# Three more first layer blocks on split data, and the order of loads and sums around them

## Chip, cores and metric

One core of one Trainium2 chip runs the kernel as a single launch. The metric is the device time of that launch in microseconds (us), lower is better. The kernel before takes 1257.91 us (median of three runs).

## The reference, cut to what matters

Three stages: a linear attention with a decaying state, then a mixture of four two-layer ReLU networks weighted per token, then one two-layer network with g = h cos h.

```python
for t in range(S):                                   # 768 steps, 4 sequences x 8 heads, head size 48
    cur = einsum('bhd,bhe->bhde', u * k[:, :, t], v[:, :, t])
    y[:, :, t] = einsum('bhd,bhde->bhe', r[:, :, t], state + cur)
    state = w[..., None] * state + einsum('bhd,bhe->bhde', k[:, :, t], v[:, :, t])
x = y as 3072 tokens x 384
for e in range(4):                                   # w1: 384 x 1024, w2: 1024 x 384
    out += p[:, e:e+1] * (maximum(x @ w1[e], 0) @ w2[e])
h = out @ w_in                                       # 384 x 2048
return (h * cos(h)) @ w_out                          # 2048 x 384
```

## The kernel before, in words

The 3072 tokens are six tiles of 512. The hidden units of both networks are cut into blocks of 128. An **item** is one block on one token tile: an up product (384 to 128, three matmuls over `kk`, lines 619 to 630), an activation, and a down product (128 to 384, three matmuls, lines 701 to 705). Eight items make a unit and accumulate in three PSUM tiles `a0` to `a2`, which VectorE evicts with the token probabilities `pb` (lines 722 and 725). The main loop runs over the item number `n` from 0. In loop step `n` stand the up product of item `n` and the down product of an item two before (`lag`); item 8's down product, in step 10, is the first to write `a0` to `a2` anew, so it needs them evicted.

Products are taken in two ways. A *split* item keeps each float32 operand as two parts, high and low (`xh`, `xl`; `w[:, 0]`, `w[:, 1]`; `gh`, `gl`), and each matmul is three: high by high, high by low, low by high. A *plain* item multiplies the float32 data as it was loaded (`raw_w`, `x_raw`). Only items 0 to 7, the first eight first layer blocks on half a token tile (256 columns), can be plain; `SPLIT` names those of them that aren't. The parts of a weight tile are made by ScalarE (high, line 522) and by VectorE or GpSimd (low, line 526), in `w_split`; those of the first tokens by `split` (lines 117, 118).

The up products go in turn to two PSUM tiles `hp0` and `hp1`. An item's up product can start when the activation of the item two before has been read out of the same tile: `gh` by ScalarE (lines 637, 641), and for split items `gl` by VectorE (line 642). The attention's matmuls use the same tiles: `a_visit` in step `n` writes into the one that item `n` doesn't use, `ups2[1 - item[0] % 2]`.

The attention is worked through in 24 cells of 128 steps of one sequence. Cells 0 and 1 come before the loop; cell `c` from 2 on is begun in step `ONE_AT[c]` (3, 6, 10, 14, ...). Its preparation is a list of steps in `steps_of`: loads `a_load_tok`, `a_load_t`; `a_ru`, `a_kt` on GpSimd; `a_r`, `a_rk`, `a_kp`, `a_sum` on VectorE. `BEGIN` holds the cells whose loads and `a_ru` don't follow the rule. `mix` places these steps between the matmuls of an item. The attention's output goes to DRAM (`yd`, line 419) and comes back transposed (`x_in`, line 432), and is split into `xh`, `xl` from the list `later`.

The order on every engine is written by hand (`tc.manual_schedule`), so each engine and each DMA queue takes its instructions in program order. DMAs are issued by SyncE (SP) or ScalarE; an issue that has to wait holds up all that stands behind it in that queue. Two orders matter here:

- The raw blocks of items 0 to 7 have tiles of their own. The first six are loaded by SP ahead of the loop, the seventh and eighth by ScalarE in steps 3 and 4.
- Later weight tiles (`w_keys`) go through `st_p`, which has three buffers `s`. `w_loads(k)` issues loads up to the k-th, `w_splits(k, eng)` splits up to the k-th. In steps 3 to 7 these stand at the head of a step, `w_loads(n - 1)` and `w_splits(n - 3, ...)`. The load of a tile has to wait until the tile three before it has been split.

```python
            if 3 <= n < BLK:
                w_loads(n - 1)
                w_splits(n - 3, nc.gpsimd if n % 2 else None)
...
            if n == 7:
                prob_get(0, 0)
```

`prob_get` (line 858) loads the first `pb`; it stands behind the `w_loads` of step 7 in SP's queue.

Of the kernel before, what the change touches and what calls it, by code (L numbers as in the profile page):

```python
# [26 lines left out]
def attention_moe_cos_mlp_kernel(  # L27
# [17 lines left out]
    nc = tc.nc  # L45
# [79 lines left out]
    def a_load_t(c):  # L125
        b, i = cells[c]
        t = ld_p.tile([128, 2, HP, 128], F32, tag="rkt", name="rkt", bufs=4)
        (nc.scalar if N_FIRST < c < 6 else nc.sync).dma_start(out=t, in_=rkt[b, i])
        ld.setdefault(c, {})["t"] = t
# [21 lines left out]

    def a_ru(c):
        for ch in range(2):
            t = ld[c]["tok"][:, ch]
            nc.gpsimd.tensor_tensor(out=t, in0=t, in1=uu_ch[:, ch], op=ALU.mult)
# [10 lines left out]
    def a_kp(c):  # L166
        t, k0 = kps[c % 3], 1 if c < N_FIRST else 2
        nc.vector.tensor_tensor(
            out=t.rearrange("q (a p d) -> q a p d", a=2, d=D), in0=ld[c]["tok"][:, k0:k0 + 2], in1=wk_ch, op=ALU.mult,
        )  # L170
        ld[c]["kp"] = t
# [263 lines left out]
    def x_split(src, j, lag, cols=slice(0, TB), step=None):  # L435
        for kk in range(KD):
            later.append((
                lag + (step or X_STEP)[kk],
                lambda kk=kk: split(xh[j][:, kk, cols], xl[j][:, kk, cols], src[:, kk, cols]),
            ))  # L440

# [21 lines left out]
    BEGIN = {3: ((a_ru, 3),), 4: ((a_load_tok, 3), (a_load_t, 4), (a_ru, 5)), 5: ((a_load_tok, 6), (a_load_t, 7), (a_ru, 8))}  # L463

    def steps_of(c):
        at, p = ONE_AT[c], ONE_AT[c - 1]
        wide = at - p > 3
        two = ONE_AT.get(c - 2, 0)
        yield from BEGIN.get(c, ((a_load_tok, two - 1), (a_load_t, two), (a_ru, p - (2 if wide else 1))))
        yield from ((a_kt, p), (a_r, p + wide), (a_rk, p + 2), (a_kp, p + 2), (a_sum, p + 2 + wide))  # L470
# [278 lines left out]
    later = []  # L749
    NEXT = {(0, False): (2, 0), (1, False): (5, 1), (2, True): (0, 0), (3, True): (1, 2)}  # L750
# [124 lines left out]
    SPLIT = (4, 5)  # L875
# [45 lines left out]
    with tc.manual_schedule():  # L921
# [16 lines left out]
        raw_load(5)  # L938
        prob_load()
# [42 lines left out]
        for n in range(NI + 4):  # L982
            live = n < NI
            moe2 = False
            if 2 < n < 5:
                raw_load(n + 3, nc.scalar)
            if 3 <= n < BLK:
                w_loads(n - 1)
                w_splits(n - 3, nc.gpsimd if n % 2 else None)
            if n == 1:  # L990
                pt = table()
                for a in range(2):
                    table2(pt, a)
                for c in range(N_FIRST + 1):
                    a_kp(c)
# [62 lines left out]
            if n < N_ATT:  # L1058
                extra += steps.pop(n, [])
            for d in [x for x in later if x[0] <= 0]:  # L1060
                extra.append((on_pe_call, d[1]))
            later = [(x[0] - 1, x[1]) for x in later if x[0] > 0]
            mix(main, extra)
            for f in ends:
                f()
            if n == 1:
                for f in (a_load_tok, a_load_t):
                    f(N_FIRST + 1)
                w_split((0, 0, SPLIT[0]), nc.gpsimd, True)
            if n == 2:  # L1070
                w_loads(1)
                for kk in range(KD):
                    split(*(t[0][:, kk, 0:N_FIRST * 128].rearrange("q (c t) -> q c t", c=N_FIRST) for t in (xh, xl)), x_raw[:, :, kk, :])
                w_split((0, 0, SPLIT[1]), nc.gpsimd, True)
            if live:
                g = unit_at[ps, un]
                if n >= BLK:
                    w_splits(min(BLK * (g + 1) + w_ahead(n, g), n - 3 if n < BLK + 3 else len(w_keys)), nc.gpsimd if n < 28 and n % 2 else None)
# [219 lines left out]
```

## Time and profile before

| what | us |
|---|---|
| runs | 1256.98, 1257.91, 1258.26 |
| the profiled execution's own time | 1257.54 |
| its span | 1255.8 |
| PE busy | 1245.1 (99%) |
| PEld busy | 1038.3 (83%) |
| DVE busy | 765.7 (61%) |
| ACT busy | 491.6 (39%) |
| POOL busy | 228.3 (18%) |

PE is TensorE's matmuls and PEld its weight loads, DVE is VectorE, ACT ScalarE, POOL GpSimd, SP SyncE; ACTq and SPq are the DMA issues of a queue. The span is first to last instruction; 1.7 us of the profiled execution's time lie around it. L619 is line 619. In a timeline row the first number is the start in us from the span's start, the second the length, and a bracket gives the engine's idle time just before and what ended it.

### The profile page before, as it was taken

To read this page: it belongs to the slowest core of one execution; us is meant where nothing else is said; L and a number is where in the kernel's file an instruction comes from. 1 tells how busy PE (TensorE), PEld (TensorE's weight loads), DVE (VectorE), ACT (ScalarE), POOL (GpSimd) and SP (SyncE) were. 2 spreads that over 40 slices of the span, in tenths; PEclk is the share of its full clock that TensorE was granted. 3 is DMA by queue.
4 is the path that set the end of the run, shared out by engine and by line. 5 is a ranking of instruction groups with operands and counts; after the bars stand their busy time and mean duration, and the time that the engine had idled before them with its cause. 6 is when DMAs were issued, how large, how long until landed. Compare 5 with 4: busy or idle time off the path is not lost.

```text
span 1255.8 us, 20628 instructions
## 1 busy us (share of the span) xinstructions
PE 1245.1 (99%) x8465; PEld 1038.3 (83%) x8465; DVE 765.7 (61%) x1265; ACT 491.6 (39%) x881; POOL 228.3 (18%) x307
## 2 busy tenths in 40 slices
PE   9999999999999999999999999999999999999997
PEld 6998888888888888888888888888888888888886
DVE  7887746766265464547645642226777677777665
ACT  5442312223211131112111221126776777766774
POOL 5885324521100000111111111122000000010100
PEclk9999999999999999999999999999999999999999
DMA  8745534344231343223321410123001400160601
GB/s 312 233 125 177 192 122 156 124 142 132 80 112 64 97 134 97 74 70 130 113 83 52 142 34 9 59 99 103 1 1 51 151 26 26 45 203 5 200 11 44
DMA packets 72502, 126.54 MB, mean 101 GB/s; under 512 B 23153, under 2 KB 44754, under 8 KB 72402
## 3 DMA queue, kind: packets, MB, share of 16 engines
q1 hardware_dynamic: 66066, 94.56, 23.6%
q0 software_dynamic: 4608, 25.17, 6.2%
q10 hardware_dynamic: 1728, 5.44, 1.3%
q8 instruction: 67, 1.10, 0.4%
q14 instruction: 33, 0.27, 0.1%
HBM read 101.90 MB, written 23.25 MB: 100 GB/s over the span
## 4 chain that ended last, share of the span: by engine, by line


## 5 line engine op out<-in xcount | busy, mean ns | idle before, releaser
L628 PE MATMUL hp<-xh,w 128*128 128x512 f32 (+1 forms) x894 | 343.1, 384 | 0.1
L629 PE MATMUL hp<-xl,w 128*128 128x512 f32 (+1 forms) x894 | 340.2, 380 | 0.0
L630 PE MATMUL hp<-xh,w 128*128 128x512 f32 (+1 forms) x894 | 339.9, 380 | 0.0
L703 PE MATMUL a<-gh,w 128*128 128x512 f32 (+1 forms) x886 | 337.6, 381 | 0.1
L704 PE MATMUL a<-gh,w 128*128 128x512 f32 (+1 forms) x886 | 336.9, 380 | 0.0
L705 PE MATMUL a<-gl,w 128*128 128x512 f32 (+1 forms) x886 | 336.8, 380 | 0.0
L641 ACT ACTIVATE gh<-hp 128x512 fp32r<-128x512 f32 (+1 forms) x202 | 114.9, 569 | 533.8 <-PE hp L630 528.3
L642 DVE SCALAR_TENSOR_TENSOR gl<-hp,gh 128x512 fp32r<-128x512 f32 (+1 forms) x202 | 132.4, 655 | 293.8 <-ACT gh L641 292.9
L628 PEld LDWEIGHTS hp<-xh,w 128*128 128x128 f32 x894 | 168.1, 188 | 33.2 <-DVE gl L642 0.3
L630 PEld LDWEIGHTS hp<-xh,w 128*128 128x128 f32 x894 | 168.1, 188 | 31.8
L629 PEld LDWEIGHTS hp<-xl,w 128*128 128x128 f32 x894 | 168.2, 188 | 31.2
L703 PEld LDWEIGHTS a<-gh,w 128*128 128x128 f32 x886 | 166.7, 188 | 32.7 <-DVE pm L725 0.7
L705 PEld LDWEIGHTS a<-gl,w 128*128 128x128 f32 x886 | 166.7, 188 | 31.6
L704 PEld LDWEIGHTS a<-gh,w 128*128 128x128 f32 x886 | 166.7, 188 | 31.5
L727 POOL TENSOR_TENSOR acc<-acc,pm 128x256 f32<-128x256 f32 x108 | 87.9, 849 | 520.3 <-DVE pm L725 520.3
L661 DVE SCALAR_TENSOR_TENSOR hs<-rr,hs 128x512 f32<-128x512 f32 x96 | 66.9, 697 | 62.6 <-ACT rr L660 62.6
L659 ACT ACTIVATE rr<-rr 128x512 f32<-128x512 f32 x96 | 60.8, 633 | 87.6 <-DVE rr L654 87.6
L653 DVE SCALAR_TENSOR_TENSOR rr<-ni,hs 128x512 f32<-128x512 int32 x96 | 66.9, 697 | 45.7 <-ACT ni L652 45.7
L530 POOL DMA_DIRECT2D w<-dec_all x32 | 17.1, 535 | 330.8 <-PE a L705 330.8
L654 DVE SCALAR_TENSOR_TENSOR rr<-ni,rr 128x512 f32<-128x512 int32 x96 | 66.9, 697 | 3.3
L118 DVE TENSOR_TENSOR gl<-hs,gh 128x512 fp32r<-128x512 f32 x96 | 65.6, 684 | 0.7 <-ACT gh L117 0.7
L651 ACT ACTIVATE hs<-hp 128x512 f32<-128x512 f32 x96 | 57.1, 595 | 17.9 <-PE hp L630 17.7
(169 smaller groups left out, 1068.7 us busy)
## 6 DMA issues: line engine op xcount, KB each, us to landing
w<-dec_all POOLq DMA_DIRECT2D x32, 768.0 KB, 4.5
s<-in_moe_wb_dram SPq DMA_DIRECT2D x53, 384.0 KB, 4.2
draw<-in_moe_wb_dram SPq DMA_DIRECT2D x32, 384.0 KB, 3.8
dec_all<-dout SPq DMA_DIRECT2D x32, 384.0 KB, 3.0
tok<-in_tok_ch_dram SPq DMA_DIRECT2D x19, 576.0 KB, 5.6
rkt<-in_rkt_dram SPq DMA_DIRECT2D x21, 512.0 KB, 3.6
pb<-pn SPq DMA_DIRECT2D x24, 256.0 KB, 5.0
out_dram<-acc SPq DMA_DIRECT2D x17, 256.0 KB, 2.8
```

Source lines behind the costliest of these rows:

```text
L628: nc.tensor.matmul(hp, wh[:, kk, :], x_h[:, kk, :], start=kk == 0, stop=False)
L629: nc.tensor.matmul(hp, wh[:, kk, :], x_l[:, kk, :], start=False, stop=False)
L630: nc.tensor.matmul(hp, wl[:, kk, :], x_h[:, kk, :], start=False, stop=kk == KD - 1)
L641: nc.scalar.activation(out=gh, in_=hp, func=ACTF.Relu)
L642: nc.vector.scalar_tensor_tensor(out=gl, in0=hp, scalar=0.0, in1=gh.bitcast(F32), op0=ALU.max, op1=ALU.subtract)
L653: nc.vector.scalar_tensor_tensor(out=rr, in0=ni, scalar=-PI2_HI, in1=hs, op0=ALU.mult, op1=ALU.add)
L654: nc.vector.scalar_tensor_tensor(out=rr, in0=ni, scalar=-PI2_LO, in1=rr, op0=ALU.mult, op1=ALU.add)
L661: nc.vector.scalar_tensor_tensor(out=hs, in0=rr, scalar=1.0, in1=hs, op0=ALU.subtract, op1=ALU.mult)
L703: nc.tensor.matmul(a, wh[:, ds], gh, start=q == 0, stop=False)
L704: nc.tensor.matmul(a, wl[:, ds], gh, start=False, stop=False)
L705: nc.tensor.matmul(a, wh[:, ds], gl, start=False, stop=q == BLK - 1)
L727: nc.gpsimd.tensor_tensor(out=o[:, x:x + 256], in0=o[:, x:x + 256], in1=m[:, x:x + 256], op=ALU.add)
```

## The change

`SPLIT` becomes (3, 4, 5, 6, 7): items 3, 6 and 7 (the fourth, seventh and eighth block) turn from plain to split, in up and down product. With that:

- Their weights are split: item 3's low part by VectorE at the head of step 1, item 5's now by VectorE in step 2 (it was GpSimd's), item 6's by GpSimd at the end of step 3, item 7's by VectorE in step 4. Item 4's stays on GpSimd, a step later.
- The first tokens are split at the end of step 1 (it was step 2), ahead of the probabilities' sums on VectorE.
- `w_splits(n - 3)` becomes `n - 4` in steps 3 to 11: the split of a later weight tile comes one step later; the `w_loads` stay.
- The seventh raw block is loaded by SP ahead of the loop, in front of the probabilities; the eighth in step 3.
- Cell 3: its `a_kt` goes to VectorE, its `a_ru` to the end of step 2. Cell 2's `a_kp` goes to GpSimd. Cell 4's `rkt` is loaded by SP, not ScalarE. The loads and `a_ru` of cells 9 and 10 are placed by hand.
- The sum `a_sum` of cells from 4 on, and the last of the three splits of the second token tile, are put behind all else of their step (`behind`).

```diff
-        (nc.scalar if N_FIRST < c < 6 else nc.sync).dma_start(out=t, in_=rkt[b, i])
+        (nc.scalar if c in (3, 5) else nc.sync).dma_start(out=t, in_=rkt[b, i])
...
+    def a_kt_v(c):
+        a_kt(c, nc.vector)
+
...
-    def a_kp(c):
+    def a_kp(c, eng=None):
         t, k0 = kps[c % 3], 1 if c < N_FIRST else 2
-        nc.vector.tensor_tensor(
+        (eng or nc.vector).tensor_tensor(
...
+        if (j, lag) == (1, XT_LAG):
+            last_x.append(later[-1][1])
...
-    BEGIN = {3: ((a_ru, 3),), 4: ((a_load_tok, 3), (a_load_t, 4), (a_ru, 5)), 5: ((a_load_tok, 6), (a_load_t, 7), (a_ru, 8))}
+    BEGIN = {3: (), 9: ((a_load_tok, 21), (a_load_t, 21), (a_ru, 25)), 10: ((a_load_tok, 21), (a_load_t, 26), (a_ru, 28)), 4: ((a_load_tok, 3), (a_load_t, 4), (a_ru, 5)), 5: ((a_load_tok, 6), (a_load_t, 7), (a_ru, 8))}
...
-        yield from ((a_kt, p), (a_r, p + wide), (a_rk, p + 2), (a_kp, p + 2), (a_sum, p + 2 + wide))
+        kt = (a_r, p + wide), (a_kt_v if c == 3 else a_kt, p)
+        yield from (*(kt if c == 3 else kt[::-1]), (a_rk, p + 2), (a_kp, p + 2), (a_sum, p + 2 + wide))
...
-    SPLIT = (4, 5)
+    SPLIT = (3, 4, 5, 6, 7)
...
         raw_load(5)
+        raw_load(6)
         prob_load()
...
-            if 2 < n < 5:
-                raw_load(n + 3, nc.scalar)
+            if n == 3:
+                raw_load(7, nc.scalar)
+            if n == 4:
+                w_split((0, 0, 7), early=True)
             if 3 <= n < BLK:
                 w_loads(n - 1)
-                w_splits(n - 3, nc.gpsimd if n % 2 else None)
+                w_splits(n - 4, nc.gpsimd if n % 2 else None)
             if n == 1:
+                w_split((0, 0, 3), early=True)
                 pt = table()
                 for a in range(2):
                     table2(pt, a)
-                for c in range(N_FIRST + 1):
+                a_kp(N_FIRST, nc.gpsimd)
+                for c in range(N_FIRST):
                     a_kp(c)
...
+            behind = [f for f in extra if f[0] is a_sum and f[1] > N_FIRST + 1]
+            extra = [f for f in extra if f not in behind]
             for d in [x for x in later if x[0] <= 0]:
-                extra.append((on_pe_call, d[1]))
+                (behind if d[1] in last_x else extra).append((on_pe_call, d[1]))
             later = [(x[0] - 1, x[1]) for x in later if x[0] > 0]
             mix(main, extra)
+            for f, c in behind:
+                f(c)
...
             if n == 1:
+                for kk in range(KD):
+                    split(*(t[0][:, kk, 0:N_FIRST * 128].rearrange("q (c t) -> q c t", c=N_FIRST) for t in (xh, xl)), x_raw[:, :, kk, :])
                 for f in (a_load_tok, a_load_t):
                     f(N_FIRST + 1)
-                w_split((0, 0, SPLIT[0]), nc.gpsimd, True)
             if n == 2:
+                w_split((0, 0, 4), nc.gpsimd, True)
                 w_loads(1)
-                for kk in range(KD):
-                    split(*(t[0][:, kk, 0:N_FIRST * 128].rearrange("q (c t) -> q c t", c=N_FIRST) for t in (xh, xl)), x_raw[:, :, kk, :])
-                w_split((0, 0, SPLIT[1]), nc.gpsimd, True)
+                a_ru(N_FIRST + 1)
+                w_split((0, 0, 5), early=True)
+            if n == 3:
+                w_split((0, 0, 6), nc.gpsimd, True)
             if live:
                 g = unit_at[ps, un]
                 if n >= BLK:
-                    w_splits(min(BLK * (g + 1) + w_ahead(n, g), n - 3 if n < BLK + 3 else len(w_keys)), nc.gpsimd if n < 28 and n % 2 else None)
+                    w_splits(min(BLK * (g + 1) + w_ahead(n, g), n - 4 if n < BLK + 4 else len(w_keys)), nc.gpsimd if n < 28 and n % 2 else None)
```

ScalarE in steps 1 and 2, before (`gh` are the activations of items 0, 1, 2; `raw_xh2` holds the raw blocks of items 4 and 5, `raw_xl1` those of items 2 and 3; `wk_ch` is the table that all `a_kp` need):

```order
L637 ACTIVATE gh_362<-hp0_352 128x256
L830 ACTIVATE wk_ch_108<-px_364 64x384 x2
L637 ACTIVATE gh_377<-hp1_353 128x256
L137 DMA tok_379<-in_tok_ch_dram 128x1152
L128 DMA rkt_381<-in_rkt_dram 128x1024
L522 ACTIVATE w_383<-raw_xh2_102 128x768
L637 ACTIVATE gh_400<-hp0_352 128x256
```

and of the change:

```order
L643 ACTIVATE gh_363<-hp0_353 128x256
L528 ACTIVATE w_365<-raw_xl1_101 128x768
L837 ACTIVATE wk_ch_108<-px_368 64x384 x2
L643 ACTIVATE gh_381<-hp1_354 128x256
L117 ACTIVATE xh0_98<-acc2_106 128x256 x3
L137 DMA tok_389<-in_tok_ch_dram 128x1152
L128 DMA rkt_391<-in_rkt_dram 128x1024
L643 ACTIVATE gh_405<-hp0_353 128x256
L528 ACTIVATE w_413<-raw_xh2_102 128x768
```

The high part of item 3's weights now stands ahead of the table, and the tokens' high parts ahead of cell 3's loads and of item 2's activation.

VectorE in steps 2 to 5, before (`s_496` is cell 2's mask step, `gl_535` item 4's low part, `w_520` the first later weight tile):

```order
L347 COPY_PREDICATED s_496<-eye_110,dsum_346 128x512
L145 TENSOR_TENSOR rkt_381<-rkt_381,pw_111 128x512
L526 TENSOR_TENSOR w_520<-s_408,w_520 128x768
L642 SCALAR_TENSOR_TENSOR gl_535<-hp0_352,gh_534 128x256
L159 TENSOR_TENSOR tok_379<-tok_379 128x384
```

and of the change (`gl_520` and `gl_548` are those of items 3 and 4):

```order
L532 TENSOR_TENSOR w_422<-raw_xh2_102,w_422 128x768
L306 TENSOR_TENSOR acc1_105<-px_434,acc1_105 48x384 x2
L345 TENSOR_TENSOR s_504<-pair_ps_128,mask_107 128x512
L350 COPY_PREDICATED s_504<-eye_110,dsum_347 128x512
L145 TENSOR_TENSOR rkt_391<-rkt_391,pw_111 128x512
L150 TENSOR_TENSOR rkt_391<-rkt_391,pw_111 128x512
L648 SCALAR_TENSOR_TENSOR gl_520<-hp1_354,gh_519 128x256
L532 TENSOR_TENSOR w_531<-raw_xl2_103,w_531 128x768
L648 SCALAR_TENSOR_TENSOR gl_548<-hp0_353,gh_547 128x256
L162 TENSOR_TENSOR tok_389<-tok_389 128x384
```

Item 5's weights, cell 3's `a_kt`, item 3's `gl` and item 7's weights are new in this stretch; `w_520` has left it.

SP's queue in steps 5 to 10, before, with what each issue waits for (`s` are later weight tiles, `s_667` the sixth; `pb_674` is the first probability tile; DMAHW is the end of an earlier DMA):

```order
L511 DMA s_667<-in_moe_wb_dram 128x768 [waits DMAHW3_49]
L858 DMA pb_674<-pn_136 128x4x128 [waits DMAHW4_49,DMAHW2_49]
L858 DMA pb_693<-pn_136 128x4x128 [waits DMAHW5_49]
L511 DMA s_718<-in_moe_wb_dram 128x768 [waits DMAHW6_49,Activation_49,Pool_49]
L137 DMA tok_725<-in_tok_ch_dram 128x1152 [waits DMAHW7_49,PE_49]
L511 DMA s_748<-in_moe_wb_dram 128x768 [waits DMAHW0_49,DVE_49]
L419 DMA yd0_646<-yt_813 48x4x64 [waits DMAHW1_49,Activation_49]
```

and of the change (`s_694` is the sixth later tile, `pb_701` the first probability tile, `s_900` the eighth later tile):

```order
L517 DMA s_694<-in_moe_wb_dram 128x768 [waits DMAHW2_49,DMAHW3_49,Activation_49,Pool_49]
L865 DMA pb_701<-pn_136 128x4x128 [waits DMAHW4_49]
L865 DMA pb_728<-pn_136 128x4x128 [waits DMAHW5_49]
L137 DMA tok_762<-in_tok_ch_dram 128x1152 [waits DMAHW6_49,PE_49]
L517 DMA s_793<-in_moe_wb_dram 128x768 [waits DMAHW7_49,DVE_49]
L422 DMA yd0_669<-yt_858 48x4x64 [waits DMAHW0_49,Activation_49]
L422 DMA yd0_669<-yt_858 48x4x64 [waits DMAHW1_49]
L422 DMA yd0_669<-yt_858 48x4x64 [waits DMAHW2_49,DVE_49]
L422 DMA yd0_669<-yt_858 48x4x64 [waits DMAHW3_49]
L128 DMA rkt_876<-in_rkt_dram 128x1024 [waits DMAHW4_49,PE_49]
L517 DMA s_900<-in_moe_wb_dram 128x768 [waits DMAHW5_49,Pool_49]
```

The sixth later tile, in front of the first `pb`, now waits for ScalarE and GpSimd as well: the third later tile, whose buffer it takes, is split in the same step 7 and no longer in step 6. The eighth has moved from before cell 4's output `yd` to behind it and behind a `rkt` load.

## Rows read from the trace of the kernel before

**Rows 1.** Busy time per engine in stretches; last PEclk, DMA share, GB/s.
```profile
10.00:15.00 5.00, 4.61 (x109) 3.80 (x110) 3.37 (x8) 2.56 (x7) 2.70 (x4) 1.00 1.04 397
300.00:400.00 100.00, 100.00 (x502) 82.65 (x501) 46.17 (x86) 21.48 (x37) 9.13 (x12) 1.00 0.29 93
```
**Rows 2.** PE's waits over the span: us in total, times, longest.
```profile
PE hp L374 <- DVE gl L642: 0.7, 1, 0.7
PE pair_ps L193 <- POOL rkt L150: 0.3, 1, 0.3
...
PE hp L619 <- DVE gl L642: 0.2, 1, 0.2
```
**Rows 3.** Timeline of PE, 35 to 40 us: plain and split products.
```profile
35.14 1.46 PE L619 MATMUL hp<-acc,raw_xl 128*128 128x256 f32 x6
36.25 0.47 PE L703 MATMUL a<-gh,w 128*128 128x256 f32 x1
...
37.51 0.28 PE L628 MATMUL hp<-xh,w 128*128 128x256 f32 x1
...
38.59 1.46 PE L701 MATMUL a<-gh,raw_xl 128*128 128x256 f32 x6
```
**Rows 4.** Timeline of ACT, 18 to 20 us: item 4's weights.
```profile
18.67 0.84 ACT L522 ACTIVATE w<-raw_xh 128x768 fp32r<-128x768 f32 x1 [0.97 <-DMA raw_xh<-in_moe_wb_dram]
```
**Rows 5.** Timeline of DVE, 16 to 33 us.
```profile
16.91 1.50 DVE L168 TENSOR_TENSOR kp<-tok,wk_ch 128x384 f32<-128x384 f32 x3 [0.66 <-ACT wk_ch L830]
19.81 0.28 DVE L843 TENSOR_REDUCE p_s<-acc 96x32 f32<-96x128 f32 x1 [1.41 <-DMA acc<-in_moe_domain_probs_dram]
...
21.10 1.07 DVE L118 TENSOR_TENSOR xl<-acc,xh 128x256 fp32r<-128x256 f32 x3
22.41 1.12 DVE L303 TENSOR_TENSOR acc<-px,acc 48x384 f32<-48x384 f32 x2 [0.24 <-ACT acc L301]
...
25.34 0.98 DVE L145 TENSOR_TENSOR rkt<-rkt,pw 128x512 f32<-128x512 f32 x1
26.53 0.98 DVE L526 TENSOR_TENSOR w<-s,w 128x768 fp32r<-128x768 f32 x1 [0.20 <-ACT w L522]
...
29.68 1.07 DVE L159 TENSOR_TENSOR tok<-tok 128x384 f32<-128x384 f32 x1 [0.30 <-DMA s<-in_moe_wb_dram]
...
32.04 0.41 DVE L642 SCALAR_TENSOR_TENSOR gl<-hp,gh 128x256 fp32r<-128x256 f32 x1
```
**Rows 6.** Timeline of PE: cell 2's visit, item 8's down product, cell 4's visit.
```profile
32.51 0.25 PE L374 MATMUL hp<-s,tok 64*48 64x64 f32 x1
...
45.39 0.28 PE L703 MATMUL a<-gh,w 128*128 128x256 f32 x1
...
55.01 0.22 PE L374 MATMUL hp<-s,tok 64*48 64x64 f32 x2
```
**Rows 7.** Timeline of SP's DMA issues, 38 to 50 us.
```profile
38.77 2.64 SPq L858 DMA_DIRECT2D pb<-pn  x2
42.31 0.35 SPq L511 DMA_DIRECT2D s<-in_moe_wb_dram  x1
...
47.80 2.31 SPq L419 DMA_DIRECT2D yd<-yt  x4
```
**Rows 8.** DMA issues at 38.8, 42.3 and 51.6 us: KB each, us to landing.
```profile
pb<-pn SPq DMA_DIRECT2D x1, 256.0 KB, 5.3
s<-in_moe_wb_dram SPq DMA_DIRECT2D x1, 384.0 KB, 4.5
acc<-yd SPq DMA_DIRECT2D x1, 384.0 KB, 3.6
```
**Rows 9.** Timeline of DVE, 44 to 48 us.
```profile
44.16 1.09 DVE L722 TENSOR_TENSOR acc<-a,pb 128x256 f32<-128x256 f32 x3 [2.17 <-DMA pb<-pn]
45.67 0.69 DVE L398 TENSOR_TENSOR yt<-px,yt 48x512 f32<-48x512 f32 x1 [0.42 <-ACT yt L393]
```
**Rows 10.** Timeline of DVE, 98 to 108 us.
```profile
105.14 0.54 DVE L163 TENSOR_REDUCE dsum<-tok 128x8 f32<-128x384 f32 x1
```

More of the change, by code (lines that the diff above doesn't have):

```diff
@@ L749, in attention_moe_cos_mlp_kernel @@
     later = []
+    last_x = []
     NEXT = {(0, False): (2, 0), (1, False): (5, 1), (2, True): (0, 0), (3, True): (1, 2)}
```

## The prediction

> **What bounds the kernel now.** I read the table of stretches first. TensorE (PE) is busy for 100.00 of 100 us in the middle of the run, at full clock [rows 1]; its work is fixed there, so whatever time PE loses or gains near the start is kept to the end. Next, PE's own waits: outside the first 14 us they are few and short, and they end with a low part `gl` on VectorE, with GpSimd's `a_kt`, or with `gl` again [rows 2]: 0.7 + 0.3 + 0.2 = 1.2 us. So the most that better order can give back is about 1.2 us. Last, the timelines of the other engines between 16 and 56 us, where VectorE, ScalarE, GpSimd and SP feed the first items; there the question is which of them will be late once the change has put more on them.
>
> A measurement of this kernel can tell about 0.2%, 2.5 us, from no change.
>
> **The products themselves.** A plain group (three matmuls, shown as six) starts at 35.14 and the next group at 36.25, 1.11 us later. That next group, nine split matmuls, takes until 37.51, 1.26 us; nine split matmuls behind another split group take 37.51 to 38.59, 1.08 us [rows 3]. The 0.18 us more is the plain group's tail, so a plain group costs 1.29 us and a split one 1.08. Three items have six such groups: 6 x 0.21 = **1.3 us saved** on PE.
> [...]
>
> **VectorE's chain up to cell 2's visit.** Item 3's weights have to be split early, and their load is the fourth of a row. The fifth ended when ScalarE could start on it, at 18.67 [rows 4]; 384 KB (0.39 MB) at the 397 GB/s of that time [rows 1] take 1.0 us, so the fourth landed at about 17.6. ScalarE now waits for it ahead of the table `wk_ch`, and VectorE, which began the three `a_kp` at 16.91, can do nothing before. From there VectorE has, in the new order and with durations from [rows 4, 5]:
> - high part on ScalarE 0.84, low part 0.98: 19.4
> - two `a_kp` (0.50 each): 20.4. The third is on GpSimd, beside this, and is needed only by cell 2's state products, behind the others.
> - the tokens' low parts 1.07: 21.5; the probabilities, 19.81 to 21.10, 1.29: 22.8
> - item 5's low part 0.98: 23.8
> - state sums, mask, copy and `a_r` as before, 22.41 to 26.32, 3.91: 27.7
> - `a_kt` on VectorE 0.98, taken from its neighbour of the same size: 28.7; `gl` of item 3 0.41; item 7's weights 0.98; `gl` of item 4 0.41: 30.5
> - `a_rk`, `a_kp`, `a_sum`, 29.68 to 32.04, 2.36: 32.8; `gl` of item 5 0.41: **33.3**
>
> Item 5's `gl` ended at 32.45 before, and the products of cell 2's visit into `hp1` started on that, at 32.51 [rows 6]. So PE is 0.85 us late there, whatever it gained or lost on the way: the waits of [rows 2] at `a_kt` and at item 6's up product are inside this and count no more. Of the saving, three and a third groups lie behind this point, 0.7 us. Net **+0.15 us** at item 8's down product (45.39 before [rows 6]). Below: three operations of 128 by 384 on VectorE took 0.50 each at 16.91 and one took 1.07 at 29.68 [rows 5]; if the two of the last cell that are as long as that go as at 16.91, 1 us less. Above: the eighth raw block, which ScalarE and so `gl` of item 4 now wait for, comes a microsecond late: 1 us more.
>
> **SP's queue: the first probabilities.** Before, the sixth later weight load and the first `pb` were issued one after the other, `pb` at 38.77 [rows 7]; it took 5.3 us [rows 8], and VectorE stood idle for 2.17 us until it could evict `a0` to `a2` at 44.16 [rows 9]. The first eviction ended at 44.16 + 0.36; PE needed it at 45.39, so there was 0.87 us in hand. Now the sixth load waits until GpSimd has made the low part of the third later tile, and that operation stands where another of the same kind stood, behind cell 4's `a_kt`: the load that waited for that one before was issued at 42.31 [rows 7]. With mask and sums of cell 3 on VectorE no earlier than before (33.3 + 0.98 for a weight tile: 34.3), I leave it there. The issue takes 0.35, so `pb` is issued at 42.7, 3.9 us later than before. To landing it takes 3.6 to 5.3 us [rows 8]; I take 4.5, what the load took that was issued at the same moment. `pb` lands at 47.2; first eviction ended 47.6, PE at 47.6 instead of 45.39: **+2.2 us** (it contains the 0.15). Bounds 3.6 and 5.3: +1.3 and +3.0; GpSimd being sooner is a rival.
> Behind the evictions VectorE has the sum of cell 4 (moved here), cell 3's output, the mask of cell 4 and its state, so these too come 47.2 - 44.16 = 3.0 us later, with the sum (0.54 [rows 10]) and less the 0.42 us that VectorE was idle there [rows 9]: +3.1 us. I count nothing for other work of ScalarE here: its activations are all ahead of their need while PE waits.
>
> **SP's queue: the eighth later tile.** It is now issued behind cell 4's `yd` (four issues, 47.80 to 50.11 before [rows 7], which wait for that mask and output) and a `rkt` load. With +3.1: `yd` from 50.9 to 53.2, the `rkt` issue some 0.4 (my estimate, from 0.35 for the one issue at 42.31), the load at 53.6; landing 3.6 later [rows 8] (the load that stood behind a `rkt` issue in the same way), 57.2. ScalarE's queue has the high part of this tile ahead of item 13's activation, and VectorE has its low part ahead of item 13's `gl`: 0.84 + 0.98 + 0.41: 59.5. Cell 4's visit, in step 14, writes into `hp1`, which item 13 used: PE starts it at 59.5 instead of 55.01 [rows 6]: **+4.5 us** in all. Bounds: 3.6 to 4.5 for this landing on top of those of `pb`, +2.9 to +6.2.
>
> **Later.** The sum of a cell (0.54 us [rows 10]) and the last token split now stand behind item 31's `gl`, on which the longest of PE's waits ended [rows 2]; that wait goes: **-0.7 us**. Cells 9 and 10 load earlier; they are off PE's path and no row shows PE waiting for them: 0, hidden by PE's own items. SP issues them when their buffers are free, which if late would hold up a `yd` behind them that is not read until items later.
>
> **Sum.** 1257.54 us (profiled execution, 0.37 below the median of the runs) + 4.5 - 0.7 = **1261.3 us**; own range 1259 to 1264.
>
> **Rivals.**
> - *The first `pb` isn't late.* GpSimd reaches the third later tile sooner, or the queue, emptier than before, lands the tile in time. Then only the eighth tile remains: `yd` at 47.80 as before, load at 50.5, landed at 54.1, `gl` of item 13 ended 56.3, PE +1.3 at cell 4's visit, less 0.7: **1258.2**, no change. It decides if `pb` lands before 45.0. For it: less stands in SP's and ScalarE's queues then. Against: GpSimd's place behind `a_kt`, and 5.3 us for this very transfer.
>  [...]
> - *Nothing is late* (faster). VectorE had 0.66 + 1.41 + 0.24 + 0.20 + 0.30 = 2.8 us of idle time between 16 and 30 us [rows 5], and if the added work fits and both loads come before their use, the saving stands whole: -1.3 - 1.2: **1255.0**. The place is SP's queue at step 7; it decides if GpSimd ends the third tile by 40. Against it: that tile can't begin before cell 4's `a_kt`.
> - *VectorE's chain is the worse wait.* Items 3 to 6 each stand for `gl`, because the eighth raw block lands after 29 us and ScalarE takes item 4's activation behind it: two more microseconds by 45 us, of which `pb`'s lateness hides one: **1263**.
> - That the change doesn't do what it says is excluded: the order of PE has 27 split matmuls more in up and in down products where the plain ones stood.
>
> **How the numbers follow.** Forecast 0.48, the worse chain 0.12: both slower by over 0.2%, 0.60. First rival 0.27, no change. Nothing late 0.13, faster. The range takes in the forecast's bounds and the first rival, and leaves out most of the last: 1255.4 to 1264.4.
>
> **What would show it.** In the changed profile: nine-matmul groups of 1.08 us in items 3, 6, 7; VectorE idle until about 18.5 us; SP's first `pb` issue near 42.7 instead of 38.77, behind a load that waited for GpSimd; VectorE idle for over 4 us up to its first eviction, and PE waiting there at line 709; then ScalarE waiting for a load ahead of item 13's activation and PE waiting at line 377 near 59 us; no wait near 106 us. The forecast is wrong if `pb` is issued before 40 us, or if PE has no wait between 44 and 60 us.

## The result, and the profile after

The changed kernel takes **1265.55 us** (median of six runs, 1263.95 to 1266.59) against 1257.57 us before (median of six, 1256.98 to 1258.26): 1.0063 times as long, 95% interval 1.0052 to 1.0074. It is slower, as forecast, but by 8.0 us and not by 3.8, and above the range's end of 1264.4.

The profiled execution took 1266.59 us, 9.05 more than that of before. First TensorE's waits of the changed kernel (total us, times, longest):

```profile
PE hp L377 <- DVE gl L648: 2.9, 1, 2.9
PE a L709 <- DVE acc L728: 2.3, 1, 2.3
PE hp L634 <- DVE gl L648: 2.1, 2, 1.7
...
PE hp L635 <- DVE xl L118: 1.1, 1, 1.1
PE a L711 <- issue: 0.8, 1, 0.8
```

Where [rows 2] had 0.7 at most, there are now 2.9 at cell 4's visit (line 377) and 2.3 at item 8's down product (line 709), the two places that the prediction named. The waits at lines 634 and 635 lie ahead of cell 2's visit, all but 0.4 us, and are VectorE's chain. Its timeline gives the lateness at each place; the rows are the first products into `hp` of the visits of cells 2, 4 and 5, and between them item 8's:

```profile
34.27 0.22 PE L377 MATMUL hp<-s,tok 64*48 64x64 f32 x2
...
48.82 0.35 PE L709 MATMUL a<-gh,w 128*128 128x256 f32 x1 [2.25 <-DVE acc L728]
...
62.36 0.34 PE L377 MATMUL hp<-s,tok 64*48 64x64 f32 x1 [2.93 <-DVE gl L648]
...
75.77 0.22 PE L377 MATMUL hp<-s,tok 64*48 64x64 f32 x2
```

Before, they stood at 32.51, 45.39 and 55.01 [rows 6], and cell 5's visit in the same view at

```profile
65.89 0.22 PE L374 MATMUL hp<-s,tok 64*48 64x64 f32 x2
```

So the changed kernel is late by 1.76, 3.43, 7.35 and 9.88 us. Between cells 4 and 5 TensorE waits for nothing that is late, and still loses 2.5 us. The table of stretches tells why (us; then busy time and instructions of PE, PEld, DVE, ACT, POOL; granted clock, DMA share, GB/s):

```profile
60.00:62.00 2.00, 0.00 (x0) 0.00 (x0) 0.99 (x2) 1.11 (x2) 0.00 (x0) 0.89 0.33 127
62.00:64.00 2.00, 1.64 (x62) 1.65 (x62) 1.97 (x4) 0.00 (x0) 0.00 (x0) 0.50 0.01 2
64.00:66.00 2.00, 2.00 (x18) 1.86 (x12) 0.90 (x3) 1.65 (x6) 0.36 (x1) 0.50 0.00 0
66.00:68.00 2.00, 2.00 (x11) 2.00 (x11) 1.97 (x5) 0.61 (x2) 1.92 (x4) 0.50 0.46 92
68.00:70.00 2.00, 2.00 (x18) 2.00 (x17) 2.00 (x3) 0.38 (x1) 2.00 (x3) 0.91 0.83 187
```

After it had stood idle for 2.93 us, TensorE was granted a clock of 0.50, half clock, from 61.6 to 68.4 us. Before, its clock was 1.00 in all of these stretches. The idle time of 2.25 us at item 8 was followed by nothing of the kind: from 48 to 60 us the clock is 1.00.

VectorE's timeline shows what was late:

```profile
19.58 1.83 DVE L171 TENSOR_TENSOR kp<-tok,wk_ch 128x384 f32<-128x384 f32 x2
21.34 1.64 DVE L118 TENSOR_TENSOR xl<-acc,xh 128x256 fp32r<-128x256 f32 x3
...
33.74 0.41 DVE L648 SCALAR_TENSOR_TENSOR gl<-hp,gh 128x256 fp32r<-128x256 f32 x1
...
48.25 1.09 DVE L728 TENSOR_TENSOR acc<-a,pb 128x256 f32<-128x256 f32 x3 [5.02 <-DMA pb<-pn]
...
61.01 0.96 DVE L532 TENSOR_TENSOR w<-s,w 128x768 fp32r<-128x768 f32 x1 [3.92 <-ACT w L528]
61.88 0.42 DVE L648 SCALAR_TENSOR_TENSOR gl<-hp,gh 128x256 fp32r<-128x256 f32 x1
```

The two `a_kp` took 1.83 us together, where each took 0.50 in [rows 5]; item 5's `gl` ends at 34.15 (before 32.45); VectorE is idle for 5.0 us until `pb` lands; item 13's `gl` waits for the eighth later tile. GpSimd's timeline has cell 4's `a_kt` and the third later tile, SP's the issues behind it, the last row being the eighth tile's load:

```profile
38.73 2.10 POOL L150 TENSOR_TENSOR rkt<-rkt,pw 128x256 f32<-128x256 f32 x2
40.80 3.16 POOL L532 TENSOR_TENSOR w<-s,w 128x256 fp32r<-128x256 f32 x3
```
```profile
43.99 0.35 SPq L517 DMA_DIRECT2D s<-in_moe_wb_dram  x1
44.38 0.98 SPq L865 DMA_DIRECT2D pb<-pn  x2
...
53.97 0.39 SPq L128 DMA_DIRECT2D rkt<-in_rkt_dram  x1
54.45 0.44 SPq L517 DMA_DIRECT2D s<-in_moe_wb_dram  x1
```

The low part ends at 43.96, and only then are the sixth tile and `pb` issued. Before, `pb` was issued at 38.77 [rows 7].

### The profile page after: what moved, and what is told of

Same layout as the page of the kernel before. It is cut to its first block, busy times and chain, and to the rows that moved or that the text cites. A ratio compares the mean times of both kernels' runs of the same rounds, so it can differ in the third digit from the quotient of the medians.

```text
span 1264.9 us, 20672 instructions
## 1 busy us (share of the span) xinstructions
PE 1246.9 (99%) x8483; PEld 1040.0 (82%) x8483; DVE 770.7 (61%) x1271; ACT 493.7 (39%) x884; POOL 229.2 (18%) x306
## 4 chain that ended last, share of the span: by engine, by line
## 5 line engine op out<-in xcount | busy, mean ns | idle before, releaser
L634 PEld LDWEIGHTS hp<-xh,w 128*128 128x128 f32 x903 | 170.3, 189 | 36.6 <-DVE gl L648 3.1
L709 PEld LDWEIGHTS a<-gh,w 128*128 128x128 f32 x895 | 168.7, 188 | 35.1 <-issue 2.4
L636 PEld LDWEIGHTS hp<-xh,w 128*128 128x128 f32 x903 | 170.2, 189 | 32.0
L710 PEld LDWEIGHTS a<-gh,w 128*128 128x128 f32 x895 | 168.7, 189 | 31.4
```

The lines of the kernel that those rows point to most:

```text
L634: nc.tensor.matmul(hp, wh[:, kk, :], x_h[:, kk, :], start=kk == 0, stop=False)
L636: nc.tensor.matmul(hp, wl[:, kk, :], x_h[:, kk, :], start=False, stop=kk == KD - 1)
L709: nc.tensor.matmul(a, wh[:, ds], gh, start=q == 0, stop=False)
L710: nc.tensor.matmul(a, wl[:, ds], gh, start=False, stop=False)
```

## Experiments

The theory: two loads stand in SP's queue behind waits that the later splits brought, and all else follows from that. The rivals: VectorE and GpSimd have too much work, since three more blocks are split; and, for the stretch at half clock and for what came after 100 us, causes of their own.

### The first `pb` ahead of the sixth tile

```diff
+            if n == 7:
+                prob_get(0, 0)
             if 3 <= n < BLK:
                 w_loads(n - 1)
...
-            if n == 7:
-                prob_get(0, 0)
```

> The changed kernel with one load moved: the first probability tile is issued ahead of the sixth later weight tile. Queue theory (the late pb comes from standing behind that weight load): pb is issued by 39.5 instead of 44.4 us and lands by 44.5; the 2.4 us wait of TensorE at 46.3 goes, VectorE's evictions, cell 4's output and with them the eighth later tile come 3 us earlier, so the wait of 3.1 us at cell 4's visit shrinks by 1 to 2 us and the low clock after it (62 to 68.5 us) is shorter or gone: 1259 to 1262 us in place of 1265.5. Load theory (VectorE and GpSimd are behind whatever the queue does, since three more blocks are split there): the wait at 46.3 is taken by another one within 2 us of it, 1264 to 1266 us.

Measured: 1265.49 us (1264.47 to 1266.04). `pb` is issued at 39.6, but lands at 46.45, 6.9 us later (expected 44.5). The wait at item 8 falls from 2.3 to 0.4 us, cell 4's visit begins at 60.09 instead of 62.36, cell 8's is 3.4 us sooner than in the changed kernel: by its places the queue's order counts. By its time the run lies where the load theory had it, for TensorE then stands for 2.05 us at 112 us, in the middle of cell 9's visit, for nothing that a semaphore shows ("issue"), goes at half clock for a stretch behind that (mean granted clock 0.91 from 100 to 120 us), and the gain is gone.

### The eighth tile ahead of cell 4's output

```diff
-                    w_splits(min(BLK * (g + 1) + w_ahead(n, g), n - 4 if n < BLK + 4 else len(w_keys)), nc.gpsimd if n < 28 and n % 2 else None)
+                    w_splits(min(BLK * (g + 1) + w_ahead(n, g), n - 3 if n < BLK + 3 else len(w_keys)), nc.gpsimd if n < 28 and n % 2 else None)
```

> The changed kernel with the splits of the later tiles a step sooner again from step 8 on only, so that the eighth tile is loaded ahead of cell 4's output; the first probability tile stays late. Queue theory: the wait at 46.3 us stays (2.4 us), item 13's low part no longer waits for a load, the 3.1 us wait at cell 4's visit goes and with it the stretch at half clock (2.5 us lost between the visits of cells 4 and 5): 1265.5 - 3.1 - 2.5 = 1259.9, within 1.5. Load theory: GpSimd and VectorE end the same splits no sooner, the load comes at the same time and the time stays within 1 us of 1265.5.

Measured: 1263.76 us (1262.54 to 1265.41). The wait at cell 4's visit is gone, `pb`'s stays at 2.0 us, with half clock behind it (0.50 from 50 to 52 us); cell 8's visit is 5.3 us sooner than in the changed kernel, near the 5.6 expected. Again some 2.2 us are lost by "issue", in the same products of cell 9's visit, so the time misses the 1259.9 expected.

### All later splits a step sooner

```diff
-                w_splits(n - 4, nc.gpsimd if n % 2 else None)
+                w_splits(n - 3, nc.gpsimd if n % 2 else None)
```

together with the edit above.

> The changed kernel with the splits of the later tiles a step sooner again everywhere, as before the change; the three more split blocks stay. Queue theory: pb is issued near 40 us, the eighth tile ahead of cell 4's output; against that VectorE has a later tile's low part (1.1 to 1.4 us) ahead of the low parts of items 4 and 5, so cell 2's visit is 1.4 us later than 34.3: 1265.5 - 2.4 - 3.1 - 2.5 + 1.4 = 1258.9, between 1257 and 1261. Load theory: VectorE and GpSimd, now asked for more by 40 us, lose there what the queue gives back: 1263 us or more.

Measured: 1262.16 us (1260.26 to 1263.40). Both waits of SP's making are gone and cell 2's visit is 1.2 us later than in the changed kernel, both as the queue theory has it: at cell 9's visit the kernel is only 1.0 us behind the kernel before. The rest, 4.3 us, is lost there, by a stop of 2.7 us from one product to the next and by half clock behind it (mean granted clock 0.91 from 100 to 120 us), and the time misses the 1257 to 1261 expected. Its PE timeline:

```profile
108.45 0.22 PE L388 MATMUL hp<-rkt,st 48*48 48x64 f32 x1
111.14 0.25 PE L388 MATMUL hp<-rkt,st 48*48 48x64 f32 x1 [2.47 <-issue]
```

In this kernel, in the two above and in the changed one (0.3 us at 116.7) TensorE stands behind the 20th or 21st of 32 products of line 388. The changed kernel had stood once more, at 111.95, which is 127 matmuls ahead in its program. So the place belongs to the program. The traces have DMA transfers of the kind "instruction", 16 KB each, on queue 8 (67 of them, 1.10 MB in all, in that of the changed kernel). Of 108.6 to 109.8 us the DMA view of this kernel shows one (packets, MB, share of 16 engines' time):

```profile
q8 instruction: 1, 0.02, 4.9%
```

4.9% of 16 engines times 1.2 us is 0.94 us. It starts at 108.8, ends at 109.7, and TensorE goes on 1.4 us later.

### TensorE's idle place filled

```diff
+        if c == 4:
+            for _ in range(13):
+                nc.tensor.matmul(ps[0], wu_a, wu_b, start=True, stop=True)
```

> The changed kernel with 13 matmuls of zeros (128 by 512, bf16) put into cell 4's visit, written where the visit's first products overwrite them, just ahead of the products that TensorE waits 3.1 us for at 59.2 us. Clock theory (TensorE's clock is lowered because it stood idle, and the low clock costs 2.5 us by itself): the wait is filled, the granted clock between 61.8 and 68.5 us is 1.00 instead of 0.50, and the time is 2.5 us shorter, 1263.0 us. Rival (the low clock has another cause, or the products after the wait are late for another reason): the clock still falls or the time stays at 1265.5; if the fill is longer than the wait, up to 0.5 us more.

Measured: 1267.67 us (1264.45 to 1268.06). This tells nothing of the clock: in the profiled run `pb` took 5.7 us to land, TensorE stood for 4.2 us at item 8, the half clock followed that (0.50 from 50 to 55 us), and at cell 4 there was no idle place to fill. Up to that load the program is the changed kernel's own, where `pb` took 3.8 us: the same transfer differs by 1.9 us between two executions. On the kernel with `pb` first the same edit (11 matmuls) meets the wait:

> The run with the first probability tile issued first, and 11 matmuls of zeros (128 by 512, bf16) at the head of cell 4's visit, where that run's TensorE stood for 2.6 us and then went at half clock to 64.5 us. Clock theory (it fell because TensorE stood idle): the place is filled, the clock stays at 1.00 from 55 to 70 us, and the first products of the visits of cells 4 and 5 are 10.9 us apart, as in the kernel before, instead of 12.2. Rival (the clock falls for another reason, or the products there are late by themselves): 1.2 us or more stay. The whole time may not show it (a stop near 112 us is as long as the blocks of the program make it): 1263 to 1266 us.

Measured: 1262.82 us (1261.83 to 1264.25). The stretches of 60 to 65 us, of the kernel with `pb` first and of the filled one:

```profile
60.00:65.00 5.00, 4.91 (x82) 4.83 (x82) 4.69 (x10) 2.26 (x7) 2.40 (x4) 0.66 0.19 39
```
```profile
60.00:65.00 5.00, 5.00 (x97) 4.92 (x87) 4.70 (x9) 2.64 (x8) 2.72 (x4) 1.00 0.28 51
```

The clock stays at 1.00. The first `hp` products of cells 4 and 5 stand at 60.09 and 72.32 without, at 59.77 and 70.68 with the fill: 12.23 and 10.91 us, and 10.88 in the kernel before. So it was the idle time that lowered the clock there, with the same work behind it, and this cost 1.3 us; in the changed kernel, with the longer idle time, 2.5. Not every idle time does it. In the kernel with the eighth tile ahead of cell 4's output, 2.04 us at item 8 were followed by half clock (0.50 from 50 to 52 us) and 2.19 us at cell 9's visit were not (1.00 from 100 to 120 us); nor were the 2.25 us at item 8 of the changed kernel (1.00 from 48 to 60 us). What tells these apart no run here shows.

### The late part alone, on the kernel before

`behind` and the loads of cells 9 and 10 as in the change; nothing else.

> The kernel before with the late part of the change alone: sums of cells and the last split of the second token tile behind all else of their step, cells 9 and 10 loaded as in the change. If that part does what the prediction said, TensorE's wait of 0.90 us at 105.8 us goes and nothing comes for it: 1257.5 - 0.9 = 1256.6 us. Rival (the wait only changes its name: TensorE then stands there for its own instructions, as the kernels with the change do at their cell 9): 1257.5 to 1260 us, with an idle time of TensorE near 106 to 109 us that no semaphore ends.

Measured: 1256.46 us (1256.20 to 1258.08), 0.9992 of before (0.9983 to 1.0001). The 0.9 us wait for `gl` is gone, and so is a stop of 0.6 us at 88 us that the kernel before had; but the rival is right on the place too: TensorE stands there for its own instructions. TensorE's timeline, and the "instruction" transfer of 105.5 to 107 us:

```profile
106.52 0.40 PE L632 MATMUL hp<-xh,w 128*128 128x512 f32 x1
108.20 0.28 PE L705 MATMUL a<-gh,w 128*128 128x256 f32 x1 [1.28 <-issue]
```
```profile
q8 instruction: 1, 0.02, 3.9%
```

3.9% of 16 x 1.5 us is 0.94 us, from 105.9 to 106.8; TensorE goes on 1.4 us after it. So this loss needs none of the three more split blocks.

### The stop moved in the program

```diff
-    GAP = 4
+    GAP = 64
```

on the kernel with all later splits a step sooner.

> The run with all later splits a step sooner, and 60 more matmuls of zeros (128 by 64, some 29 ns each) at the start of step 2, where TensorE goes on to wait for the tokens' low parts (1.4 us) and for a low part (1.9 us). It moves every later matmul 60 places on in TensorE's program. Theory of blocks (TensorE stands at 108.5 us because a 16 KB block of its program, 128 pairs of weight load and matmul, has not arrived at that place of the program): the stop of 2.5 us leaves its place behind the 20th of the 32 last products of cell 9's visit, to 60 matmuls before, and is shorter than 1.5 us or gone: 1262.2 - 1 to 4 = 1258 to 1261. Theory of time (whatever stops it belongs to that moment, as a transfer or another engine would): it stays in the same products for over 2 us, 1262 to 1263.

Measured: 1262.29 us (1260.31 to 1266.62). Cell 9's visit has no stop any more; there are others, of 0.4 us at 83.1, 0.8 at 102.7 and 2.85 us at 57.8, where the half clock follows (mean granted clock 0.66 from 60 to 65 us). Counted from the start of the trace, these stops come behind 984, 1366 and 1748 matmuls, 382 apart, which is about three times 127 (127.3 to a block by this count, where the expectation had 128 pairs); the changed kernel's two come behind 1749 and 1876. The theory of blocks is right on the place, and wrong on what that brings: a stop in one place is traded for one in another, and the time stays.

### Loads moved away from the stop

```diff
...
+    ... 11: ((a_load_tok, 28), (a_load_t, 32), (a_ru, 31)), 12: ((a_load_tok, 32), (a_load_t, 32), (a_ru, 34)), ...
```

in `BEGIN`, on the same kernel.

> The run with all later splits a step sooner, and two loads that fill the DMA engines from 104 to 109 us (rkt of cell 11, tokens of cell 12, 1.1 MB) put behind the next cell's output, after 112 us. If the 16 KB block of TensorE's program is late because it queues behind those loads: it starts 1.5 to 2 us sooner than 108.8, TensorE's stop at 108.5 us falls from 2.5 us to under 1, and the time by 1.5 to 3 us, less what cell 11 then waits for its rkt (up to 2 us a little after 120 us). If the block is asked for late, and the loads don't matter: the stop stays at 2.0 us or more.

Measured: 1264.39 us (1264.11 to 1265.07). The DMA view of 106 to 108 us, whose first row is the DMA engines' busy share in 40 slices of 0.05 us (the block, 1.06 us long, counts in the slice in which it starts):

```profile
DMA  0000000000009000000000000000000000000000
...
q8 instruction: 1, 0.02, 3.3%
```

The block is alone there, starts at 106.6 (2.2 us sooner than 108.8), and the stop falls from 2.7 to 0.3 us: the block was late behind the loads. The time rises all the same, where 1.5 to 3 us less were expected, for cell 11's rkt is now late by more than was allowed for; VectorE stands for it, and behind that operation a `gl` on which TensorE waits for 4.2 us, with half clock behind that (mean granted clock 0.96 from 115 to 120 us):

```profile
117.37 0.69 DVE L145 TENSOR_TENSOR rkt<-rkt,pw 128x512 f32<-128x512 f32 x1 [5.85 <-DMA rkt<-in_rkt_dram]
```

### Three blocks plain again

`SPLIT = (4, 5)`, and without the splits of items 3, 6 and 7.

> The changed kernel with the fourth, seventh and eighth block plain again, so without their split weights and low parts; loads, sums and the later splits stay where the change puts them. Load theory (VectorE and GpSimd are late because three more blocks are split): no wait of TensorE over 0.5 us at 46 and at 59 us, no half clock; 1265.5 - 2.4 - 3.1 - 2.5 + 1.3 = 1258.8, within 1.5. Queue theory (the later tiles split a step later are the cause, whatever is split early): pb is still issued after 42 us and the eighth tile behind cell 4's output, so half or more of both waits stays: 1262 to 1266 us.

Measured: 1260.99 us (1257.20 to 1264.74). Both waits stay: 1.9 us at item 8 and 1.8 at cell 4, with half clock behind each (mean granted clock 0.67 from 45 to 50 us and 0.66 from 60 to 65 us). So the waits don't need the three blocks, and at cell 4 the load theory falls. At item 8 it doesn't: TensorE was 1.4 us ahead of the kernel before at cells 2 and 3, came to the wait sooner, and left it only 0.69 us behind that kernel (46.08 against 45.39), not 3.43. `pb` was issued at 39.54 here, not after 42, and landed 5.9 us later. The kernel before issued it at 38.77, the kernel with the three blocks and all later splits a step sooner at 41.61, the changed kernel at 44.38. So its late issue takes both: the low part of the third later tile stands behind cell 4's `a_kt` by the later split, and ends on GpSimd at 39.12 without the three blocks' work and at 43.96 with it.

### Cell 2's keys on VectorE again

```diff
-                a_kp(N_FIRST, nc.gpsimd)
-                for c in range(N_FIRST):
+                for c in range(N_FIRST + 1):
```

> The changed kernel with cell 2's keys (the third of the products with the table) on VectorE again instead of GpSimd. If VectorE was slower there because GpSimd read beside it (0.92 us each where the kernel before took 0.50): the three take 1.5 us in all where the two took 1.83, the tokens' low parts, three of 128 by 256, 1.1 to 1.4 us where they took 1.64, and the visit of cell 2 begins 0.3 to 0.9 us sooner than 34.27. If the two engines don't disturb each other: VectorE has one more of 0.9 us, and the visit begins 0.5 to 0.9 us later.

One run: 1265.40 us. VectorE's timeline, and the visit of cell 2 on PE:

```profile
19.39 1.49 DVE L171 TENSOR_TENSOR kp<-tok,wk_ch 128x384 f32<-128x384 f32 x3
20.80 1.09 DVE L118 TENSOR_TENSOR xl<-acc,xh 128x256 fp32r<-128x256 f32 x3
```
```profile
33.20 0.23 PE L377 MATMUL hp<-s,tok 64*48 64x64 f32 x2
```

Three operations take less time than two did beside GpSimd, and the visit begins at 33.20, 1.07 us sooner than 34.27 and a little more than expected. What was gained went at once: `pb` took 5.3 us to land and TensorE waited 3.5 us at item 8.

### What the runs speak for, together

The change with all later splits a step sooner, `pb` first, these keys on VectorE, and cell 12's token load behind the next cell's output:

> The change with what the runs so far speak for: all later splits a step sooner, the first probability tile first, cell 2's keys on VectorE, cell 12's token load behind the next cell's output; three more blocks split. From the run with the splits sooner (1262.2; 1.0 us behind the kernel before at cell 9's visit, then a stop of 2.7 and 1.6 of half clock): keys -0.5, the stop to 1.0 and no half clock: 1262.2 - 0.5 - 1.7 - 1.6 = 1258.4, between 1257 and 1260. If a wait comes in the place of each as it did in the single runs: 1262 us.

Measured: 1259.00 us (1257.97 to 1260.23), 1.0011 of before (1.0002 to 1.0020): 6.5 us of the 8.0 are back, as expected, and no long wait came for those removed. The stop at cell 9's visit is 1.0 us. And the late part alone with that one load moved:

```diff
...
+    ... 12: ((a_load_tok, 32), (a_load_t, 32), (a_ru, 34)), ...
```

> The late part of the change alone on the kernel before, with cell 12's token load put behind the next cell's output, so that one load less stands on the DMA engines at 101 to 106.4 us. If the block of TensorE's program was late behind these loads (it started at 105.9 and TensorE went on 1.3 us after it had landed): it starts at 104.9, when the other load has landed, TensorE's stop of 1.45 us at 106.5 falls to 0.3 to 0.6, and the time to 1256.46 - 1.0 = 1255.5 us, the fastest here. If not: the stop stays over 1.2 us and the time at 1256.4.

Measured: **1255.77 us** (1255.12 to 1256.39), 0.9986 of before (0.9977 to 0.9995). Its DMA view of 104.5 to 106 us, and TensorE where the kernel without this edit stood from 106.52 to 108.20:

```profile
DMA  0005090000000000000000000000000000000000
...
q8 instruction: 1, 0.02, 4.4%
```
```profile
106.86 0.40 PE L632 MATMUL hp<-xh,w 128*128 128x512 f32 x1
107.10 0.28 PE L705 MATMUL a<-gh,w 128*128 128x256 f32 x1
```

The block starts 1.2 us sooner, at 104.7, and the stop is gone. This is the fastest kernel here, and none of its first layer blocks was changed.

## Why the prediction was right and wrong

- **The products themselves: right.** From cell 2's visit to cell 3's, with 0.7 us of saving forecast, the lateness falls from 1.76 to 1.02 us.
- **VectorE's chain: mechanism right, one term short.** Forecast +0.85 us at cell 2's visit, measured +1.76. The working took 0.50 us each for the two `a_kp`, from a row in which GpSimd stood idle, and counted the third, on GpSimd "beside this", as free. It wasn't: the first of the two took 0.56 us, the second, begun while GpSimd had the third, 1.36.

```profile
20.05 1.36 DVE L171 TENSOR_TENSOR kp<-tok,wk_ch 128x384 f32<-128x384 f32 x1
```
```profile
19.62 1.37 POOL L171 TENSOR_TENSOR kp<-tok,wk_ch 128x384 f32<-128x384 f32 x1 [4.34 <-ACT wk_ch L837]
```

The tokens' low parts took 1.64 us for 1.07. The row of the 1.07 had GpSimd beside it as well, but there it was GpSimd that stood: its operation in the middle took 1.81 us, the one ahead of it 0.73.

```profile
20.97 1.81 POOL L526 TENSOR_TENSOR w<-raw_xh,w 128x256 fp32r<-128x256 f32 x1
```

So in each of these pairs of rows one of the two engines took over twice as long beside the other: VectorE's second `a_kp` 1.36 us for 0.56, ending 0.4 us after GpSimd's, and GpSimd's operation 1.81 for 0.73. With all three on VectorE they took 1.49 us in all, and the visit began at 33.20; the working had 33.3 with two there, and with three would have had 33.8. What decides which of the two engines stands, no run here shows.
- **The first `pb`: mechanism right, size partly by luck.** Forecast issue 42.7, landing 47.2 and +2.2 us; measured 44.4, 48.15 and +3.4. The issue came 1.7 us later than forecast, and the transfer took 0.7 us less than the 4.5 taken; the two errors partly cancel. The third later tile ended on GpSimd at 43.96 and not at 42.3: GpSimd had become a chain of its own, which between 21.95 and 47.1 us stood idle for 0.6 us, and which the working hadn't followed.
- **The eighth later tile: the step that failed.** "Landing 3.6 later" was 5.7, by its own row of the DMA view (KB, us to landing),

```profile
s<-in_moe_wb_dram SPq DMA_DIRECT2D x1, 384.0 KB, 5.7
```

so it landed at 60.1 and not at 57.2, and cell 4's visit was 7.35 us late, not 4.5, past that term's upper bound of 6.2. Of the 2.85 us too few, 2.1 are this landing, and most of the rest comes from `pb`. The 3.6 was that of a load issued 1.4 us behind a `rkt` load of 512 KB; here 0.5 us lie between the two, and the `rkt` load had been counted as an issue of 0.4 us, and not as a transfer. In the kernel with `pb` first this load took 4.6 us; in the kernel before, where it was issued 0.5 us behind a token load of 576 KB (42.76 and 43.23), 6.0. The term's lower bound, +2.9, is +3.6 by its own parts.
- **The clock: a term that was missing.** An idle time at cell 4 of 2.3 us (4.5 less 2.2) was forecast, and 2.9 came, but not that TensorE would be granted half clock (0.50) after it: 2.5 us. The last two points are what the range lacked.
- **Later: a third of the gain.** Forecast -0.7 us. Two stops went (0.6 us at 88 and 0.9 at 105.8), 1.5 us in all; 0.9 and 0.3 us came for them where TensorE stood for its program, and -0.25 us was left. The working read three of PE's waits before and said that the most that better order could give back was 1.2 us; it passed over a row of the same view,

```profile
PE hp L385 <- issue: 0.4, 1, 0.4
```

which is the stop at 88 us, and the first sign of this limit: a block of 16 KB lands at 87.2 us, and TensorE goes on at 88.6.

In all: 7.35 + 2.5 - 0.25 = 9.6 us from cell 11's visit on, of which half a microsecond comes back at the very end. The six runs scatter more (2.6 us) than those of before (1.3); the profiled one is the slowest of them.

Of the rivals, "the first `pb` isn't late" and "nothing is late" are excluded by the waits. "VectorE's chain is the worse wait" asked for two more microseconds by 45 us; 0.9 came, for at cell 3's visit, at 44.96, TensorE was 1.02 us late and not 0.15. (Its price, 1263, is 1262.3 by its own terms.) The change was slower by the forecast's mechanism, at 7.35 us for 4.5, and by a half clock that the forecast didn't have. Why the same `pb` took from 3.8 us (the changed kernel) to 6.9 (issued first) is not settled. Two executions of programs that are the same up to it differ by 1.9 us in it; it was not alone on the DMA engines (busy share 0.89 from 40 to 45 us with `pb` first, 1.06 from 46 to 48 us in the changed kernel), and no run tells its neighbours apart.

## What to carry to other kernels

Where one queue issues loads in a fixed order, a step that delays the freeing of a buffer delays all that stands behind that load, as here `pb`, issued at 44.38 us for 38.77: follow the queue row by row, and count the load just ahead as a transfer and not as an issue (5.7 us to landing here, for the 3.6 taken). Take a duration from a row in which the same neighbours run, on the other engines too. Idle times of TensorE of 2.4 and 2.9 us cost 1.3 and 2.5 us more here, at a granted clock of 0.50, though after one of 2.25 us it stayed at 1.00; so filling an idle time with matmuls of zeros can pay, as it did with `pb` first (1265.49 to 1262.82 us). Before two operations are put side by side on VectorE and GpSimd, look in the trace at which of them would stand: here it was VectorE once (1.36 us for 0.56) and GpSimd once (1.81 for 0.73). And a wait removed in a stretch of many short matmuls may only uncover the one behind it, as the 2.05 us at 112 us with `pb` first.

## What the runs showed of the hardware

By these runs TensorE's program arrives by DMA in blocks of 16 KB. The trace of the kernel before has 67 of these transfers on queue 8 (1.10 MB), and 8465 weight loads and as many matmuls, 253 of the two together for each transfer, or 126 matmuls; no other engine has over 1500 instructions. At the stops quoted here a block took 0.9 to 1.3 us, and TensorE went on 1.2 to 1.5 us after it had landed: in the kernel with all later splits sooner (109.7, 111.1), the late part alone (106.8, 108.2), the moved program (59.5, 60.7) and the moved loads (107.7, 109.1). The changed kernel's two stops agree (111.6, 113.0 and 115.7, 117.0). Visits of cells use 128 matmuls in 1.9 us, about the 127 that lay between those two stops. The 126 of the count agree with that 127. Most of the 67 blocks pass without a stop: of TensorE's waits in the kernel before one, of 0.4 us, ends by "issue". At and just behind the visits of cells there were such stops of 0.3 to 2.85 us. What sets the moment at which a block is asked for, no run here shows.
